# The first block's taps shared out anew, and the transposes and transfers of blocks 2 and 3 moved, in a dynamic convolution followed by a two-layer product

## The chip, the cores and the metric

One Trainium2 chip, one of its eight cores. The metric is the time of one execution on the device in microseconds (us), as the median of several runs; a profile is one more execution, recorded instruction by instruction.

## The reference

x is (4, 4096, 192), weight_gen (4, 4096, 8, 7), w_in (192, 2048), w_out (2048, 192), all float32.

```
w   = softmax(weight_gen) over its 7 taps
out[b, s, h, :] = sum over k of w[b, s, h, k] * x[b, s + k - 6, h, :]     (zeros ahead of s = 0)
h   = out @ w_in                                   # 16384 tokens, 192 -> 2048
g   = h where h >= 1, 0 where h <= -1, (h + 1)^2 / 4 between
result = g @ w_out                                 # 2048 -> 192
```

## The kernel before, in words

**Blocks and pairs.** The 16384 tokens are cut into 32 blocks of 512. A block's convolution gives a tile with tokens on partitions (128 partitions, 4 tokens each, 192 channels); gemm1 wants channels on partitions, so the block is transposed and split into a rounded part hc and a rest hl (`split_x`, L256). gemm1 makes 128 columns of d_ff at a time, gemm2 sums over them. One step is one such slice of 128, and the program is written in pairs of steps: a block has 8 pairs, and the loop over w (L600) has 256 pairs of gemm1 (`gemm1_pair`, L373) and, LAGP = 2 pairs later, as many of gemm2 (`gemm2_part`, L418, two parts for each pair). Pair w = 8 is the first of block 1, w = 16 of block 2, w = 24 of block 3.

**Between the two products** ScalarE and VectorE make g from a step's sums: `relu` and `square` (ScalarE, L398, L401), `act_g` (VectorE, L406), `split_g` (ScalarE gh L412, VectorE gl L413). gemm1's sums lie in four PSUM banks of the pool ps_h, two for each pair; a bank is free when split_g has read it.

**The order of the work** is written out by hand (`tc.manual_schedule`): each engine does its instructions in program order. `at(w, op, place=p)` (L478) puts an operation into pair w. In program order a pair is gemm1, place 5, gemm2, relu and square of its first step, place 0, relu of the second, place 9, square of the second and act_g of the first, places 10 and 1, act_g of the second, the evacuation's copies, place 2, split_g of both, places 13 and 4 (L600 to L651).

**SP's queue** issues all the transfers and has a second task. In `gemm2_part` a bank passes from one half of the rows to the other, and the matmul that takes it over waits for a no-op on SP (L443) that itself waits for the matmul before. The no-ops stand on SP in program order with the transfers: a transfer that waits there holds the no-ops behind it, and so gemm2.

**The first block** (L539 to L581). `softmax(0)`, then `conv_summed(0)` (L217): KV = 3 taps are summed on VectorE with PSUM as the accumulator and end in a piece, four taps are single products of GpSimd, a piece each. A piece is a tile of 192 channels with the first 64 repeated behind by ScalarE (`again`, L168), so that channels can be read as two neighbouring halves in any of three ways. TensorE turns each piece (`turn_sum`, L267; 12 turns for one piece, 4 for each of 3 chunks of channels) and sums the five pieces in PSUM (src). `drive(n, bank)` (L206) lets TensorE do n matmuls of 512 columns on the identity that nobody reads.

**The weights** come in eight chunks and are decoded (rounded high part and rest): `load_weights(c)`, `size(c)` on ScalarE (L328), `decode(c)`: VectorE mag (L360), head (L362) and two merges (L341), then ScalarE high and VectorE low for each half (L353, L357). Chunk c is needed by pair w = c; chunks 2 to 7 are decoded in pairs 1 to 6. Block 1's convolution on GpSimd is held back behind those decodings (L587), and it is turned by TensorE too (pair 7).

**Blocks 2 and on** (L513 to L537). `conv(b, nc.gpsimd)` has 13 operations on GpSimd (7 products, L179, and 6 adds, L189). `transpose_out(b)` (L275) has five operations: VectorE transposes acc into T (L289), a store D <- T to DRAM (L291), and for each of three chunks of channels a gather of two transfers XT <- D (L286). `split_out(b)` has ScalarE's hc (L262) and GpSimd's hl (L263) for each chunk. Their places are given as lists of (pair, place); for block b they count from w = (b - 2) * 8. For blocks 2 and 3 the transpose is at (w+11, place 2), the store at (w+12, 0), the gathers at (w+12, 4), (w+13, 0), (w+13, 4), the splits at (w+14, 0), (w+14, 4), (w+15, 0). For the others the first four stand at w+8 to w+12.

**The end.** `evac(b)` (L449) adds the two halves of a block's sums in two turns (ScalarE L457, VectorE L458 each), and one store writes the block (L466).

Of the kernel before, what the change touches and what calls it, by code (L numbers as in the profile page):

```python
# [10 lines left out]
F32 = mybir.dt.float32  # L11
# [10 lines left out]
def kernel(  # L22
# [22 lines left out]
    P = 128  # L45
# [9 lines left out]
    E = H * K  # L55
    R = D // 32
    LAGP = 2
    KV = 3


    n = 4
# [38 lines left out]
    def run(ops):  # L100
        for o in ops:
            o()
# [57 lines left out]
    SYNC = mybir.DependencyInfo(mybir.DependencyClass.Sync, mybir.DependencyReason.DATA)  # L160

    def whole():
        return op.tile([P, n, D + Q], F32, tag="piece", name="piece", bufs=K - KV + 1)

    def heads(t):
        return t[:, :, 0:D].rearrange("p j (h g) -> p j h g", h=H)

    def again(t):  # L168
        nc.scalar.activation(out=t[:, :, D:D + Q], in_=t[:, :, 0:Q], func=AF.Copy)
# [47 lines left out]
    def conv_summed(b):  # L217

        g, gi = group_of[b]
        wt, xtile = w_t[g], x_t.pop(b)  # L220
        near = ps_o.tile([P, 2, 512], F32, tag="o1", name="near")
        wn = near[:, 0, 0:n * E].rearrange("p (j h k) -> p j h k", j=n, h=H)
        sums = ps_o.tile([P, 2, 512], F32, tag="o0", name="sums")
        acc = sums.rearrange("p a d -> p (a d)")[:, 0:n * D].rearrange("p (j h g) -> p j h g", j=n, h=H)
        nc.scalar.activation(out=wn, in_=wt[:, gi], func=AF.Copy)

        def times(eng, out, w, k):
            return eng.tensor_tensor(
                out=out, in0=xtile[:, k:k + n, :].rearrange("p j (h g) -> p j h g", h=H),
                in1=w[:, :, :, k:k + 1].to_broadcast([P, n, H, G]), op=ALU.mult)  # L230

        own, pooled = [whole()], []

        def add(k):
            t = cv.tile([P, n, H, G], F32, tag="T", name="tap")
            times(nc.vector, t, wn, k)
            out = acc
            if k == KV - 1:
                out = heads(own[0])
            nc.vector.tensor_tensor(out=out, in0=acc, in1=t, op=ALU.add)  # L240
            if k == KV - 1:
                again(own[0])

        def alone(k):
            t = whole()
            pooled.append(t)
            times(nc.gpsimd, heads(t), wt[:, gi], k)
            again(t)

        return ([lambda: times(nc.vector, acc, wn, 0)] + [lambda k=k: add(k) for k in range(1, KV)],  # L250
                [lambda k=k: alone(k) for k in range(KV, K)], pooled, own)


    xT_t, xs_t, lows = {}, {}, []
# [39 lines left out]
    def split_out(b, eng):  # L294
        XT = xs_t.pop(b)
        return split_x(b, [XT[:, c].rearrange("p a n -> p (a n)") for c in range(NC)], eng)
# [76 lines left out]
    def gemm1_pair(w):  # L373

        b, f = steps[2 * w]
        hc, hl = xT_t[b]
        if w == 0:
            pair = [ps_o.tile([P, 2, 512], F32, tag=f"o{m}", name="psh0")[:, 0] for m in range(2)]
        else:
            pair = [ps_h.tile([P, 512], F32, tag="h", name="psh") for _ in range(2)]  # L380
        passes = []
        for l, r in ((whi, hc), (wlo, hc), (whi, hl)):
            passes += [(l, r, c) for c in range(NC)]
        for s, (l, r, c) in enumerate(passes):
            for h in range(2):
                rows = slice(h * Q, (h + 1) * Q)
                nc.tensor.matmul(out=pair[h][:, 0:N], lhsT=l[rows, f // 2, c], rhs=r[rows, (c - h) % NC if b < 2 else c],  # L387
                                 start=(s == 0), stop=(s == len(passes) - 1))
        for h in range(2):
            h_t[2 * w + h] = pair[h]  # L390
# [58 lines left out]
    def evac(b):  # L449

        t0 = b * N
        osb = op.tile([P, 4, D], F32, tag="osb", name="osb")
        pos = o_t.pop(b)
        by_turn = osb.rearrange("p (k m) d -> p m k d", m=n // 2)
        ops = []
        for m in range(n // 2):
            ops.append(lambda m=m: nc.scalar.activation(out=by_turn[:, m], in_=pos[m][:, :, D:2 * D], func=AF.Copy))  # L457
            ops.append(lambda m=m: nc.vector.tensor_tensor(  # L458
                out=by_turn[:, m], in0=pos[m][:, :, 0:D], in1=by_turn[:, m], op=ALU.add))

        def store():
            rows = out[t0:t0 + N, :]
            if b < 2:
                nc.sync.dma_start(out=rows.rearrange("(p j) d -> p (j d)", j=n), in_=osb.rearrange("p j d -> p (j d)"))
            else:
                nc.sync.dma_start(out=rows.rearrange("(a q) d -> q a d", q=P), in_=osb)  # L466

        return ops, store

# [11 lines left out]
    def later(make, where):  # L481

        ops = []
        for k, (w, place) in enumerate(where):
            if k == 0:
                at(w, lambda: ops.extend(make()), place=place)
            at(w, lambda k=k: ops[k](), place=place)
# [25 lines left out]
    for b in range(2, NB):  # L513
        w = (b - 2) * NP
        at(max(w - 5, 2), lambda b=b: clear_x(b))
        at({2: 3, 3: 8, 4: 11}.get(b, w - 3), lambda b=b: load_x(b), place=4 if b == 4 else 2)
        if b in first and b > 2:
            g = first[b]
            at(max(w - 9, NP - 1), lambda g=g: load_w(g))
            if b == 3:  # L520
                where = [(10, 4), (11, 2), (12, 0), (12, 4), (12, 4), (12, 4), (13, 2)]
            else:
                where = [(w - 6 + k, 4) for k in range(7)]
            later(lambda g=g, b=b: softmax(g, nc.gpsimd if b == 3 else nc.vector), where)
        if b == 2:
            where = [(6, 2)] * 2 + [(7 + k // 3, 2) for k in range(2 * K - 3)]
        else:
            z, d = (13, 3) if b == 3 else (w + CONV, 2)
            where = [(z + k // d, 2) for k in range(2 * K - 1)]
        later(lambda b=b: conv(b, nc.gpsimd), where)  # L530
        turned = [(TOUT, 2)] + [(TOUT + k, 0) for k in range(1, 2 + NC)]
        where = [(SPLIT + k // 4, (0, 0, 4, 4)[k % 4]) for k in range(2 * NC)]
        if b < 4:
            turned = [(11, 2), (12, 0), (12, 4), (13, 0), (13, 4)]
            where = [(14, 0)] * 2 + [(14, 4)] * 2 + [(15, 0)] * 2
        later(lambda b=b: transpose_out(b), [(w + k, place) for k, place in turned])
        later(lambda b=b: split_out(b, nc.gpsimd), [(w + k, place) for k, place in where])  # L537

    with tc.manual_schedule():  # L539
        nc.gpsimd.memset(warm, 0.0)  # L540
# [8 lines left out]
        clear_x(1)  # L549
        s0, s1 = softmax(0), softmax(1, nc.gpsimd)  # L550
        marks = [o() for o in s0[0:3] + s1[0:2] + s0[3:]]
        load_weights(0, marks[-1])
        load_weights(1)
        load_x(1)
        load_weights(2)
        load_weights(3)
        run(s1[2:4])
        v_ops, p_ops, pooled, own = conv_summed(0)
        src = [ps_h.tile([P, 512], F32, tag="h", name="psx") for _ in range(NC)]
        idle = ps_h.tile([P, 512], F32, tag="h", name="idle")  # L560
        drive(10, idle, marks[1])
        run(p_ops[0:3])
        run(v_ops)
        size(0)
        run(p_ops[3:])
        run(s1[4:6])
        for k, t in enumerate(pooled[0:3]):
            for c in range(NC):
                turn_sum(src, t, k == 0, False, c)
            drive(1, idle)  # L570
        d_ops, moves = decode(0)
        for c in range(NC):
            turn_sum(src, own[0], False, False, c)
            turn_sum(src, pooled[3], False, True, c)
        run(d_ops[0:3])
        splits = split_x(0, src, nc.vector)
        scaled = s1[6]()
        tc.add_manual_dep(scaled.ins, dec_last[0].ins.name, SYNC, reason="the decoding of a chunk goes first")
        run(splits[0:1] + splits[2:3] + moves[0:1] + splits[1:2] + splits[4:5] + moves[1:2] + splits[3:4] + splits[5:6])
        run(d_ops[3:])  # L580
        run(moves[2:4])  # L581
        size(1)
        e_ops, e_moves = decode(1)
        at(0, *e_ops, place=0)
        move(0, e_moves)
        turned1 = whole()
        n_ops = conv(1, nc.gpsimd, lambda k: dec_last.get(1 + k // 2), turned1)  # L587
        for k in range(2 * K - 1):
            at(k // 2, n_ops[k], place=1)
        at(NP - 2, lambda: again(turned1), place=4)  # L590
        at(0, lambda: drive(14, ps_h.tile([P, 512], F32, tag="h", name="idle")), place=5)
        at(1, lambda: drive(12, ps_o.tile([P, 2, 512], F32, tag="o0", name="idle")[:, 0]), place=5)
        src1 = []

        def turn1(c):
# [4 lines left out]
        for w in range(NS // 2 + LAGP):  # L600
# [29 lines left out]
            else:  # L630
# [11 lines left out]
                run(side.pop((w, 1), []))  # L642
                if i < NS:
                    act_g(j)
                run(copies)
                run(side.pop((w, 2), []))
                if i < NS:
                    split_g(i)
                    split_g(j)
            for place in (13, 4):  # L650
                run(side.pop((w, place), []))  # L651
            if store and i >= NS:
                store()
        assert not side, side


# [28 lines left out]
```

## Time and profile before

| | |
|---|---|
| runs (three), median | 1179.7 us (1177.17 to 1182.65) |
| the profiled execution, its own time | 1180.91 us |
| its span, first to last instruction | 1179.1 us |
| mean granted TensorE clock | 0.996 |
| busy: TensorE, ScalarE, VectorE, GpSimd | 1155.3, 969.5, 839.1, 797.8 us |

Busy time is time with an instruction at work, however slowly it moves. PE is TensorE's matmuls, DVE VectorE, ACT ScalarE, POOL GpSimd, SPq the queue of SyncE. A start time counts from the first instruction of the span.

### The profile page before, as it was taken

How to read it: one execution, taken by the hardware profiler on the slowest of the kernel's cores; microseconds unless marked ns; L12 is line 12 of the kernel's file. 1: busy time of each engine (PE TensorE's matmuls, PEld its weight loads, DVE VectorE, ACT ScalarE, POOL GpSimd, SP SyncE). 2: the span in 40 equal slices, each digit the busy share in tenths (PEclk: the TensorE clock that was granted, in tenths of full speed). 3: DMA queues.
4: the chain of work that ended last, by engine and by line, in shares of the span. 5: the costliest groups of instructions: out<-in, count | busy, mean ns of one | idle time of the engine just before them, and what ended most of it. 6: DMA issues, size and time to landing. Idle time of an engine off the chain costs nothing.

```text
span 1179.1 us, 32263 instructions
## 1 busy us (share of the span) xinstructions
PE 1155.3 (98%) x12911; PEld 1040.2 (88%) x12911; DVE 839.1 (71%) x1275; ACT 969.5 (82%) x1746; POOL 797.8 (68%) x514
## 2 busy tenths in 40 slices
PE   8898999999999999999999999999999999999998
PEld 5687889999999999999999999999999999999997
DVE  7975677767677776777767677676777767667665
ACT  5876788888888888888888888888888888888886
POOL 4586878586668848677685767858667785866410
PEclk9999999999999999999999999999999999999999
DMA  9312222122222122212122221212221222221100
GB/s 227 100 56 83 76 67 81 64 83 89 88 63 79 67 73 96 89 59 83 67 87 75 88 85 59 86 67 82 89 89 62 72 73 76 92 89 55 46 19 20
DMA packets 84038, 91.45 MB, mean 78 GB/s; under 512 B 5040, under 2 KB 75696, under 8 KB 83888
## 3 DMA queue, kind: packets, MB, share of 16 engines
q1 hardware_dynamic: 83888, 89.39, 23.5%
q8 instruction: 102, 1.67, 0.6%
q14 instruction: 48, 0.39, 0.1%
HBM read 64.99 MB, written 24.38 MB: 76 GB/s over the span
## 4 chain that ended last, share of the span: by engine, by line
PE 92%; DVE 3%; ACT 2%; DMA 1%; POOL 1%; issue 1%; SPq 0%; POOLq 0%; DVEq 0%
PE o L434 47%; PE psh L387 44%; PE psx L271 1%; DVE psh L406 1%; DMA D<-T 1%; DVE psw L341 1%; DVE head L362 1%; ACT mag L328 1%; DMA x<-in_x_dram 0%; POOL hl L263 0%; DVE wlo L357 0%; ACT u L398 0%; ACT hc L262 0%; POOL acc L189 0%; ACT u L401 0%
## 5 line engine op out<-in xcount | busy, mean ns | idle before, releaser
L434 PE MATMUL o<-wo,gh 64*128 64x384 f32 x4096 | 604.6, 355 | 4.7 <-SPq L443 4.7
L406 DVE SCALAR_TENSOR_TENSOR psh<-u,psh 128x512 f32<-128x512 f32 x512 | 354.6, 696 | 310.4 <-ACT u L401 310.3
L434 PE MATMUL o<-wo,gl 64*128 64x192 f32 x4096 | 525.5, 251 | 0.0
L434 PEld LDWEIGHTS o<-wo,gl 64*128 64x128 f32 x4096 | 398.1, 188 | 10.9
L434 PEld LDWEIGHTS o<-wo,gh 64*128 64x128 f32 x4096 | 392.3, 184 | 15.7 <-SPq L443 5.2
L398 ACT ACTIVATE u<-psh 128x512 f32<-128x512 f32 x512 | 301.9, 590 | 105.8 <-PE psh L387 104.1
L413 DVE TENSOR_TENSOR gl<-psh,gh 128x512 fp32r<-128x512 f32 x512 | 345.4, 686 | 15.1 <-ACT gh L412 0.7
L412 ACT ACTIVATE gh<-psh 128x512 fp32r<-128x512 f32 x512 | 299.7, 593 | 65.5 <-DVE psh L406 65.3
L189 POOL TENSOR_TENSOR acc<-acc,pr 128x768 f32<-128x768 f32 x185 | 342.5, 1851 | 2.3
L401 ACT ACTIVATE u<-u 128x512 f32<-128x512 f32 x512 | 323.6, 632 | 16.0
L179 POOL TENSOR_TENSOR pr<-x,w 128x768 f32<-128x768 f32 x186 | 286.2, 1546 | 18.8 <-DVE psw L341 14.0
L263 POOL TENSOR_TENSOR hl<-XT,hc 128x512 fp32r<-128x512 f32 x90 | 115.3, 1294 | 210.7 <-ACT hc L262 210.7
L387 PE MATMUL psh<-hc,whi 64*128 64x512 f32 x1536 | 232.9, 402 | 7.3 <-DVE wlo L357 6.7
L387 PE MATMUL psh<-hl,whi 64*128 64x512 f32 x1536 | 222.9, 390 | 2.6 <-POOL hl L263 2.6
L387 PE MATMUL psh<-hc,wlo 64*128 64x512 f32 x1536 | 224.9, 394 | 0.0
L387 PEld LDWEIGHTS psh<-hl,whi 64*128 64x128 f32 x1536 | 147.0, 184 | 36.8 <-POOL hl L263 3.8
L387 PEld LDWEIGHTS psh<-hc,wlo 64*128 64x128 f32 x1536 | 148.3, 186 | 34.3
L387 PEld LDWEIGHTS psh<-hc,whi 64*128 64x128 f32 x1536 | 128.7, 187 | 24.3 <-DVE wlo L357 6.2
L179 POOL TENSOR_TENSOR acc<-x,w 128x768 f32<-128x768 f32 x31 | 47.9, 1546 | 83.2 <-DVE w L155 75.9
L262 ACT ACTIVATE hc<-XT 128x512 fp32r<-128x512 f32 x90 | 55.7, 618 | 0.0
L289 DVE STREAM_TRANSPOSE T<-acc 128x768 f32<-128x768 f32 x30 | 50.9, 1698 | 0.0
L458 DVE TENSOR_TENSOR osb<-o,osb 128x384 f32<-128x384 f32 x64 | 32.8, 555 | 2.3 <-ACT osb L457 2.3
(44 smaller groups left out, 214.4 us busy)
## 6 DMA issues: line engine op xcount, KB each, us to landing
x<-in_x_dram SPq DMA_DIRECT2D x28, 960.0 KB
XT<-D SPq DMA_DIRECT2D x180, 128.0 KB
out_dram<-osb SPq DMA_DIRECT2D x32, 384.0 KB
D<-T SPq DMA_DIRECT2D x30, 384.0 KB
x<-in_x_dram SPq DMA_DIRECT2D x4, 945.0 KB
w<-in_weight_gen_dram SPq DMA_DIRECT2D x15, 224.0 KB
r<-in_moe_w_in_dram SPq DMA_DIRECT2D x16, 192.0 KB
r<-in_moe_w_out_dram SPq DMA_DIRECT2D x8, 384.0 KB
```

The source lines that it names most:

```text
L179: held(eng.tensor_tensor(out=t, in0=xtile[:, k:k + n, :].rearrange("p j (h g) -> p j h g", h=H), in1=wt[:, gi, :, :, k:k + 1].to_broadcast ...
L189: held(eng.tensor_tensor(out=o, in0=s, in1=t, op=ALU.add))
L262: ops.append(lambda c=c: nc.scalar.activation(out=hc[:, c], in_=src[c], func=AF.Copy))
L263: ops.append(lambda c=c: lows.append(eng.tensor_tensor(out=hl[:, c], in0=src[c], in1=hc[:, c].bitcast(F32), op=ALU.subtract)))
L289: lambda: nc.vector.transpose(out=T.rearrange("p b c j -> p b j c"), in_=acc.rearrange("p j (r b) -> p b j r", b=R)),
L387: nc.tensor.matmul(out=pair[h][:, 0:N], lhsT=l[rows, f // 2, c], rhs=r[rows, (c - h) % NC if b < 2 else c], start=(s == 0), stop=(s == len ...
L398: nc.scalar.activation(out=u_t[i], in_=h_t[i][:, 0:N], func=AF.Relu, scale=0.5, bias=0.5)
L401: nc.scalar.activation(out=u_t[i], in_=u_t[i], func=AF.Square)
L406: nc.vector.scalar_tensor_tensor(out=pv, in0=uv, scalar=1.0, in1=pv, op0=ALU.min, op1=ALU.max)
L412: nc.scalar.activation(out=gh[:, 0:N], in_=gv, func=AF.Copy)
L413: nc.vector.tensor_tensor(out=gl[:, 0:N], in0=gv, in1=gh[:, 0:N].bitcast(F32), op=ALU.subtract)
L434: mm = nc.tensor.matmul(out=o_t[b][turn][:, k, 0:cols], lhsT=l[rows, t * P:(t + 1) * P], rhs=wo[rows, f].rearrange("p s d -> p (s d)")[:, ...
```

## The change

In the first block VectorE makes one tap (tap 0) as a product alone and sums three (taps 1 to 3); GpSimd makes three (taps 4 to 6). The five pieces are turned one after the other, with no drive between them, behind 16 drives instead of 10. The weights' first transfer waits for the softmax's exponential instead of its last product. size(1) and part of the decoding of chunks 0 and 1 change their places in the order; the 14 drives behind pair 0 go, ten stand ahead of pair 1's matmuls, six instead of twelve behind them. For blocks 2 and 3 transpose, store, gathers and splits stand half a pair to a pair sooner, and block 3's convolution is spread differently; block 4's convolution, transpose and transfers stand one pair later. The stores of blocks that are evacuated after the last gemm1 go out in two halves.

```diff
-    KV = 3
+    KV = 4
...
     def whole():
-        return op.tile([P, n, D + Q], F32, tag="piece", name="piece", bufs=K - KV + 1)
+        return op.tile([P, n, D + Q], F32, tag="piece", name="piece", bufs=5)
...
-        own, pooled = [whole()], []
+        def alone(eng, w, k):
+            t = whole()
+            times(eng, heads(t), w, k)
+            again(t)
+            return t
 
         def add(k):
             t = cv.tile([P, n, H, G], F32, tag="T", name="tap")
             times(nc.vector, t, wn, k)
             out = acc
             if k == KV - 1:
+                own.append(whole())
                 out = heads(own[0])
             nc.vector.tensor_tensor(out=out, in0=acc, in1=t, op=ALU.add)
-            if k == KV - 1:
-                again(own[0])
-
-        def alone(k):
-            t = whole()
-            pooled.append(t)
-            times(nc.gpsimd, heads(t), wt[:, gi], k)
-            again(t)
-
-        return ([lambda: times(nc.vector, acc, wn, 0)] + [lambda k=k: add(k) for k in range(1, KV)],
-                [lambda k=k: alone(k) for k in range(KV, K)], pooled, own)
+
+        own = []
+        return alone, wn, wt[:, gi], lambda: times(nc.vector, acc, wn, 1), add, own
...
+        if w == 1:
+            drive(10, pair[0])
         passes = []
...
-        def store():
+        def store(m=None):
             rows = out[t0:t0 + N, :]
...
+            elif m is None:
+                nc.sync.dma_start(out=rows.rearrange("(a q) d -> q a d", q=P), in_=osb)
             else:
-                nc.sync.dma_start(out=rows.rearrange("(a q) d -> q a d", q=P), in_=osb)
+                nc.sync.dma_start(out=rows.rearrange("(k m q) d -> q m k d", q=P, m=n // 2)[:, m], in_=by_turn[:, m])
...
             if b == 3:
-                where = [(10, 4), (11, 2), (12, 0), (12, 4), (12, 4), (12, 4), (13, 2)]
+                where = [(10, 4), (11, 2), (12, 0), (12, 4), (12, 4), (12, 4), (12, 4)]
...
+        elif b == 3:
+            where = [(13 + k // 2, 2) for k in range(6)] + [(16, 2)] * 3 + [(17, 2)] * 2 + [(18, 2)] * 2
         else:
-            z, d = (13, 3) if b == 3 else (w + CONV, 2)
-            where = [(z + k // d, 2) for k in range(2 * K - 1)]
+            where = [(w + CONV + (b == 4) + k // 2, 2) for k in range(2 * K - 1)]
         later(lambda b=b: conv(b, nc.gpsimd), where)
-        turned = [(TOUT, 2)] + [(TOUT + k, 0) for k in range(1, 2 + NC)]
-        where = [(SPLIT + k // 4, (0, 0, 4, 4)[k % 4]) for k in range(2 * NC)]
+        z = w + (b == 4)
+        turned = [(z + TOUT, 2)] + [(z + TOUT + k, 0) for k in range(1, 2 + NC)]
+        where = [(w + SPLIT + k // 4, (0, 0, 4, 4)[k % 4]) for k in range(2 * NC)]
         if b < 4:
-            turned = [(11, 2), (12, 0), (12, 4), (13, 0), (13, 4)]
-            where = [(14, 0)] * 2 + [(14, 4)] * 2 + [(15, 0)] * 2
-        later(lambda b=b: transpose_out(b), [(w + k, place) for k, place in turned])
-        later(lambda b=b: split_out(b, nc.gpsimd), [(w + k, place) for k, place in where])
+            turned = [(w + 11, 0), (w + 11, 0), (w + 12, 0), (w + 12, 0), (w + 13, 0)]
+            where = [(w + 13, 4)] * 2 + [(w + 14, 0)] * 2 + [(w + 14, 4)] * 2
+        later(lambda b=b: transpose_out(b), turned)
+        later(lambda b=b: split_out(b, nc.gpsimd), where)
...
-        load_weights(0, marks[-1])
+        load_weights(0, marks[2])
...
-        v_ops, p_ops, pooled, own = conv_summed(0)
+        alone, near, far, second, add, own = conv_summed(0)
         src = [ps_h.tile([P, 512], F32, tag="h", name="psx") for _ in range(NC)]
-        idle = ps_h.tile([P, 512], F32, tag="h", name="idle")
-        drive(10, idle, marks[1])
-        run(p_ops[0:3])
-        run(v_ops)
+        drive(16, src[0], marks[1])
+        pieces = [alone(nc.vector, near, 0), alone(nc.gpsimd, far, KV)]
+        second()
+        pieces.append(alone(nc.gpsimd, far, KV + 1))
+        add(2)
+        pieces.append(alone(nc.gpsimd, far, KV + 2))
         size(0)
-        run(p_ops[3:])
+        add(3)
+        again(own[0])
+        pieces.append(own[0])
+        size(1)
+        for k, t in enumerate(pieces):
+            for c in range(NC):
+                turn_sum(src, t, k == 0, k == len(pieces) - 1, c)
+        d_ops, moves = decode(0)
+        run(d_ops[0:3])
         run(s1[4:6])
-        for k, t in enumerate(pooled[0:3]):
-            for c in range(NC):
-                turn_sum(src, t, k == 0, False, c)
-            drive(1, idle)
-        d_ops, moves = decode(0)
-        for c in range(NC):
-            turn_sum(src, own[0], False, False, c)
-            turn_sum(src, pooled[3], False, True, c)
-        run(d_ops[0:3])
         splits = split_x(0, src, nc.vector)
+        run(splits[0:1] + moves[0:1] + splits[1:2] + moves[1:2] + splits[2:3] + splits[4:5] + splits[3:4] + splits[5:6])
         scaled = s1[6]()
...
-        run(splits[0:1] + splits[2:3] + moves[0:1] + splits[1:2] + splits[4:5] + moves[1:2] + splits[3:4] + splits[5:6])
-        run(d_ops[3:])
-        run(moves[2:4])
-        size(1)
         e_ops, e_moves = decode(1)
-        at(0, *e_ops, place=0)
-        move(0, e_moves)
+        at(0, d_ops[3], *e_ops, place=0)
+        at(0, moves[2], e_moves[0], e_moves[2], place=9)
+        at(0, moves[3], e_moves[1], e_moves[3], place=10)
...
-        at(0, lambda: drive(14, ps_h.tile([P, 512], F32, tag="h", name="idle")), place=5)
-        at(1, lambda: drive(12, ps_o.tile([P, 2, 512], F32, tag="o0", name="idle")[:, 0]), place=5)
+        at(1, lambda: drive(6, ps_o.tile([P, 2, 512], F32, tag="o0", name="idle")[:, 0]), place=5)
...
-                run(copies)
+                if i < NS:
+                    run(copies)
+                else:
+                    for m in range(n // 2 if store else 0):
+                        run(copies[2 * m:2 * m + 2])
+                        store(m)
...
-            if store and i >= NS:
-                store()
```

## Rows read from the trace of the kernel before

**Rows 1.** Chain of waits in order of time, from pair 8: start us, us, what.

```profile
69.75 2.30 PE psh L387 x17
...
91.83 0.10 PE psh L387
...
92.02 4.21 DMA D<-T
...
134.10 3.83 DMA D<-T
...
156.25 2.12 PE psh L387 x18
...
1165.30 2.12 PE psh L387 x18
```

**Rows 2.** Waits between 60 and 160 us: us in total, times, longest.

```profile
PE o L434 <- SPq L443: 4.7, 2, 2.4
...
PE psh L387 <- POOL hl L263: 2.6, 3, 1.4
```

**Rows 3.** Windows: busy us (instructions) by engine, PEclk, DMA share, GB/s.

```profile
97.50:101.75 4.25, 4.15 (x28) 3.69 (x30) 0.83 (x2) 0.11 (x1) 4.00 (x3) 0.60 0.32 94
101.75:106.14 4.39, 4.39 (x52) 3.99 (x52) 1.16 (x2) 3.35 (x6) 1.56 (x2) 1.00 0.31 88
```

**Rows 4.** The page's groups of GpSimd: busy us, mean ns, idle before.

```profile
L189 POOL TENSOR_TENSOR acc<-acc,pr 128x768 f32<-128x768 f32 x185 | 342.5, 1851 | 2.3
...
L179 POOL TENSOR_TENSOR pr<-x,w 128x768 f32<-128x768 f32 x186 | 286.2, 1546 | 18.8 <-DVE psw L341 14.0
L263 POOL TENSOR_TENSOR hl<-XT,hc 128x512 fp32r<-128x512 f32 x90 | 115.3, 1294 | 210.7 <-ACT hc L262 210.7
```

**Rows 5.** Timeline of GpSimd: start us, us, then what; idle before in brackets.

```profile
81.24 3.79 POOL L189 TENSOR_TENSOR acc<-acc,pr 128x768 f32<-128x768 f32 x2
...
95.91 0.97 POOL L155 TENSOR_TENSOR w<-w,s 128x448 f32<-128x448 f32 x1 [9.15 <-DVE s L154]
```

**Rows 6.** Timeline of VectorE in pairs 10 and 11.

```profile
85.10 0.61 DVE L149 TENSOR_REDUCE m<-w 128x64 f32<-128x448 f32 x1
...
88.12 1.66 DVE L289 STREAM_TRANSPOSE T<-acc 128x768 f32<-128x768 f32 x1
```

**Rows 7.** The gathers of tile XT on SP's queue: ns min/median/max, first and last start.

```profile
L286 SPq DMA_DIRECT2D XT<-D x180: 573/602/1933, 96.2 to 1122.2; - x180
```

**Rows 8.** Timeline of TensorE in the head.

```profile
3.73 4.43 PE L209 MATMUL idle<-ident 128*128 128x512 bf16 x10 [3.73 <-DVE w L150]
8.78 2.82 PE L271 MATMUL psx<-ident,piece 128*128 128x128 f32 x12 [0.62 <-POOL piece L228]
...
15.41 2.78 PE L271 MATMUL psx<-ident,piece 128*128 128x128 f32 x24
...
31.73 1.41 PE L387 MATMUL psh<-hc,whi 64*128 64x512 f32 x6 [1.06 <-DVE wlo L357]
```

**Rows 9.** Chain of waits in order of time, decoding of the first chunks.

```profile
21.02 0.90 ACT mag L328
...
25.04 0.46 DVE wlo L357
...
27.09 0.90 ACT mag L328
...
33.18 0.90 ACT mag L328
```

**Rows 10.** Timeline of GpSimd, VectorE and ScalarE in the first block.

```profile
7.18 6.04 POOL L228 TENSOR_TENSOR piece<-x,w 128x768 f32<-128x768 f32 x4 [1.57 <-DMA x<-in_x_dram]
...
10.87 0.96 DVE L240 TENSOR_TENSOR piece<-sums,tap 128x768 f32<-128x768 f32 x1
...
12.76 0.91 ACT L328 ACTIVATE mag<-r 128x768 bf16<-128x768 bf16 x1 [0.28 <-DMA r<-in_moe_w_out_dram]
```

**Rows 11.** Timeline of SP's queue, the last transfer.

```profile
1175.42 0.38 SPq L466 DMA_DIRECT2D out_dram<-osb  x1
```

## The prediction

> **What bounds the kernel now.** I read the engines' shares first (the table above): TensorE is busy nearly all the time. The reader should not take that as "nothing to gain", because busy is not the same as advancing at full pace. So the next view is the chain of waits in order of time [rows 1]. From the start of pair w=25 (156.25) to that of w=255 (1165.30) lie 230 pairs in 1009.05 us, 4.387 us each, and nothing but matmuls is on the chain: that part cannot become shorter by moving work about. From w=8 (69.75) to w=25 lie 17 pairs, which at 4.387 would take 74.6 us and take 86.5: **11.9 us are lost there**. The waits of that stretch say where [rows 2]: TensorE waits twice for an SP no-op (longest 2.4 us) and three times for hl of GpSimd. Both waits for SP begin behind a D store (92.02 and 134.10 [rows 1]): a gather waits on SP for the store to land, 4.21 and 3.83 us, and the no-ops that release the next half of gemm2 stand behind it. After such a gap the granted clock is low: 0.60 of full over 97.50 to 101.75 [rows 3]; at the lower level of 0.5 that makes 3.4 us at 1.2 GHz, some 1.7 us of matmul work. Before w=8 the chain is another one: turns of the first block, then decoding, which repeats every 6.09 us (27.09 to 33.18) [rows 9] while TensorE needs 4.39.
>
> **Part 1, the first block up to its last turn (call that moment E).** Now E is 15.41 + 2.78 = 18.19 [rows 8]. The change takes one product from GpSimd (four run 7.18 to 13.22 [rows 10], so 1.5 us) and gives VectorE a product (about 0.96, as its adds [rows 10]): six operations of 0.96 from 7.2 end at 12.9, and ScalarE's copy of the last piece follows by 13.5. The pieces are not the limit, TensorE is: ten drives take 4.43 (0.44 each), the first twelve turns 2.82 (0.235 each), the last 24 turns 2.78 (some 0.11 each) [rows 8]. The pace doubled between them, though TensorE had a gap of 0.62 after the drives. With 16 drives and no gap I bound the drives' end: all at the lower pace, 3.73 + 16 x 0.44 = 10.8; half of them at the doubled pace, 9.0. I take the middle, 9.9. Sixty turns at 0.109 are 6.5, so E = 16.4 (15.5 to 17.3; if the first twelve still go at the lower pace and the drives end late, 18.9). **Gain 1.8.** The three single drives between the sets go; their cost is in E. The weights' transfers are issued some 2.4 us sooner; chunk 0 landed just before 12.76, when ScalarE took it up [rows 10], so it is there in time for size(0) near 12.2 and the gain beyond that is nothing. They follow x on SP's queue; should they delay x, E moves by less than 0.5, as it hangs on the drives and not on x.
>
> **Part 2, from E to the decoding loop.** From E to size(2) at 27.09 now lie 8.9 us, and VectorE's decoding of chunk 1 in them waits for size(1) of ScalarE [rows 9]: 0.90 from 21.02, after a wait of some 0.4; then VectorE's head, merges, act_g, two lows and act_g follow. The change does size(1) under the turns, which takes 1.3 out, and puts one low (0.46, the row at 25.04 [rows 9]) into the chain: **gain 0.85**. Splitting hc0 and whi in another order gains nothing: hc2, which ends last, stays last. The ten drives before pair 1 cost nothing, since TensorE would wait there for whi of chunk 1; the cover is that wait, and without it they would cost 2.2. The 14 drives of pair 0 go. Behind pair 1 six drives stand instead of twelve. The idle time there was 1.06 (the row at 31.73 [rows 8]); six drives fewer add 1.3 and the shortened chain before pair 1's matmuls 0.8, so **some 3.2 us of idle time arise**, more than the 2.4 after which the clock fell [rows 2, 3]. I expect a fall there. Its 1.7 us of lost work lie beside 1.0 to 1.7 of slack in the 6.09 us loop: I charge 0.6 (0 if the clock holds, 2.5 if the fall lasts twice as long).
>
> **Part 3, blocks 2 and 3** (times as if the head had not moved; pair 13 starts at 91.83). Block 2: GpSimd's last add ends at 85.03 [rows 5], VectorE's max at 85.71 [rows 6], so the transpose moved to place 0 runs 85.7 to 87.4 (1.66 each [rows 6]). Behind it wait act_g and split_g of pair 11, 1.0 late, which pair 13 needs only at 91.8. SP gets to the D store after pair 11's no-ops, at 87.45, ahead of load_x(4), which now queues behind it at no cost. The store lands by 91.7; the first two gathers, now together behind pair 12's no-ops, issue four transfers of 0.60 [rows 7], to 94.3. Pair 13's second half needs its no-ops at 95.1. **The first wait goes**, with 0.8 to spare, and so does the fall behind it. GpSimd's order becomes softmax multiply (to 96.88, as now [rows 5]), two products, hl0, hl1, product, add, hl2. With 1.55, 1.85 and 1.29 [rows 4] hl2 ends at 107.25; pair 16 wants it at 106.9: 0.35 lost.
>
> Block 3: the nine convolution operations left (four products, five adds, 15.4) end at 122.7, but pair 19 starts at 118.5. **This is what is late next**: the transpose at place 0 waits on VectorE until 122.7, and pair 19's act_g, which waits behind it, ends by 126, just before pair 21 wants the banks. D is issued at 124.4 and lands near 128.4; gathers go to 130.8, and pair 21's second half wants its no-ops at 130.5. I charge 0.7 (0.3 to 1.0). Block 4's first eight operations, hl0, hl1, two more, and hl2 then end at 143.25 against 143.0 wanted: 0.25. In all 1.3 of the 11.9 remain: **gain 10.6** (6.6 if one wait still grows to 2.4 and costs a fall of the clock, together over 4; 11.9 if none is left). The softmax multiply of block 3 keeps its neighbours on GpSimd: nothing. Block 4's transpose and gathers come one pair later; its last gather may make ScalarE wait half a microsecond, once, covered by the pair it is ahead.
>
> **Part 4, the tail.** The last store is issued at 1175.42 [rows 11], and the span ends 3.7 later. Half of it now goes one VectorE add sooner: **gain 0.5** (0 to 1.0; the bytes are the same, one issue more).
>
> **The sum**: 1.8 + 0.85 - 0.6 + 10.6 + 0.5 = 13.2 off the profiled execution's 1180.9, so 1167.7. That execution is 1.2 above the median; I leave that in the range.
>
> **A rule that speaks against the gap-free turns.** The row of the last turns [rows 8] shows 0.11 each for 24 in a row after a single drive, so in this kernel turns ran, and kept running, at the doubled pace. The Trainium skill, in "TensorE: Matmul & The Clock Gate", section "Part 4: PE-mode transpose", says that transposes do not count as activity in the way matmuls do and that the full clock does not engage for them. By that rule the turns would all go at the lower pace once the drives between them are gone, the first rival below.
>
> **The rivals.**
> - *The turns stay at the lower pace.* Sixty at 0.235 are 14.1 instead of 6.5: 7.6 more, 1175.3. For it: the first twelve, which followed drives. Against it: the last 24. Chance 0.08.
> - *GpSimd becomes the bound of blocks 2 and 3, or SP's gathers still hold the no-ops.* One D store lands 1.5 later, or VectorE reaches a transpose later: one old wait and one fall stay, 4 more, 1171.7 (to 1175). For it: margins of 0.3 to 0.8. Chance 0.15, two thirds of it still faster.
> - *Slower: the clock falls in the new gap behind pair 1 and stays down while decoding lasts.* Pairs 2 to 7 then need 8.77 instead of 6.09: 6 x 2.7 = 16.1, less the 0.6 charged, 1183.2. Each pair beyond the seventh costs 4.4 more, so one suffices for clearly slower; it decides from five pairs on. Against it: at half clock TensorE would be busy without a pause, and after the falls of today the clock came back in such a stretch [rows 3]. Chance 0.04.
> - *Something the trace of before does not show in the head* (a bank that is not free, a late transfer): 0.03, slower.
>
> **How the numbers follow.** The forecast has 0.70. A measurement of this kernel can tell about 0.5% from no change, 5.9 us: faster is below 1173.8, slower above 1185.6. Faster: 0.70 + 0.10; same: 0.05 of the second rival, 0.08 of the first and 0.02 of the third; slower: 0.02 + 0.03. The forecast's own bounds are 1164.4 (all gains at their best) and, with the larger charges, 1172; the run-to-run difference takes the low end to 1163.5, and the second rival the high end to 1174.5.
>
> **What the changed profile would show.** Turns that end near 16.4, twelve in some 1.3; size(2) near 24.5; a gap of some 3 us behind pair 1 and a low granted clock after it; no wait of gemm2 for SP over 1 us; transpose of block 3 waiting for GpSimd; waits for hl of some tenths each; pairs of 4.387 from w=25 on, which starts 11 to 13 sooner. The prediction is wrong if a wait for SP of 2 us is left, if turns take 0.235 throughout, or if pairs 2 to 7 take over 6.5 each.

## The result, and the profile after

The changed kernel takes 1169.0 us (median of five runs, 1168.41 to 1170.81); the kernel before, beside it, 1179.03. The ratio is 0.9918 (95% interval 0.9896 to 0.9940): faster by 0.8%. The profiled execution took 1170.06 with a span of 1168.3, 10.8 below that of before.

Where the span went, stretch by stretch (E is the end of the first block's last turn, size(2) the start of ScalarE's first step for chunk 2, pairs by the start of gemm1), all from one execution of each:

| stretch | before | after | change | forecast |
|---|---|---|---|---|
| start to E | 18.19 | 16.85 | -1.34 | -1.8 |
| E to size(2) | 8.90 | 8.13 | -0.77 | -0.85 |
| size(2) to pair 8 | 42.66 | 43.47 | +0.81 | +0.6 |
| pair 8 to pair 25 | 86.50 | 76.36 | -10.14 | -10.6 |
| pair 25 to pair 255 | 1009.05 | 1009.92 | +0.87 | 0 |
| pair 255 to the end | 13.80 | 13.57 | -0.23 | -0.5 |
| span | 1179.1 | 1168.3 | -10.80 | -13.15 |

The chain of waits in order of time after the change, to set beside [rows 1]:

```profile
68.45 2.31 PE psh L386 x17
...
129.47 0.02 SPq L442
...
144.81 2.12 PE psh L386 x18
...
149.20 2.16 PE psh L386 x18
...
153.89 2.31 PE psh L386 x17
...
158.42 1.74 PE psh L386 x14
...
1154.73 2.12 PE psh L386 x18
```

Both pieces "DMA D<-T" have left the chain. Pair 25 starts 11.44 sooner, pair 255 10.57 sooner. The waits between 56 and 160 us, beside [rows 2]:

```profile
PEld psh L386 <- POOL hl L260: 1.5, 2, 0.9
...
DVE T L286 <- POOL acc L189: 1.2, 1, 1.2
...
PE psh L386 <- POOL hl L260: 0.7, 2, 0.4
...
PEld psh L386 <- DVE gl L412: 0.4, 1, 0.4
```

TensorE's matmuls no longer wait for an SP no-op in this list, hl costs 0.7 instead of 2.6, and there are two new waits: VectorE's transpose of block 3 for GpSimd, and a weight load for gl. GpSimd and VectorE where [rows 5, 6] showed them, then VectorE, with its rows 37 and 66 us later:

```profile
79.89 3.79 POOL L189 TENSOR_TENSOR acc<-acc,pr 128x768 f32<-128x768 f32 x2
...
94.64 0.98 POOL L155 TENSOR_TENSOR w<-w,s 128x448 f32<-128x448 f32 x1 [9.15 <-DVE s L154]
```

```profile
84.35 1.76 DVE L286 STREAM_TRANSPOSE T<-acc 128x768 f32<-128x768 f32 x1
...
121.37 1.73 DVE L286 STREAM_TRANSPOSE T<-acc 128x768 f32<-128x768 f32 x1 [1.17 <-POOL acc L189]
...
150.01 1.01 DVE L457 TENSOR_TENSOR osb<-o,osb 128x384 f32<-128x384 f32 x2
150.94 1.75 DVE L286 STREAM_TRANSPOSE T<-acc 128x768 f32<-128x768 f32 x1
152.57 1.27 DVE L412 TENSOR_TENSOR gl<-psh,gh 128x512 fp32r<-128x512 f32 x2
```

The last three rows are the price of block 4's later transpose: in pair 25 VectorE also evacuates block 2, so gl ends at 153.84, pair 27 starts 4.69 after pair 26 instead of 4.39, and pair 28 another 4.53 later (158.42): 0.45 in all. TensorE in the head, beside [rows 8], and the clock around the gap behind pair 1, beside [rows 3]:

```profile
3.79 6.51 PE L209 MATMUL psx<-ident 128*128 128x512 bf16 x16 [3.79 <-DVE w L150]
10.14 6.71 PE L268 MATMUL psx<-ident,piece 128*128 128x128 f32 x60
...
29.52 1.97 PE L386 MATMUL psh<-hc,whi 64*128 64x512 f32 x6 [2.77 <-DVE wlo L354]
```

```profile
26.75:29.50 2.75, 0.00 (x0) 0.00 (x0) 2.72 (x6) 2.29 (x6) 1.01 (x1) 1.00 1.10 188
30.25:33.50 3.25, 3.25 (x18) 2.50 (x18) 2.98 (x6) 1.42 (x2) 1.58 (x1) 0.50 0.05 13
```

Sixty turns without a drive between them take 6.71. Behind pair 1 TensorE is idle for 2.77, and then the granted clock is 0.50, 1.2 GHz. At the start of the span the granted clock in the windows is 1.00 even where one drive takes over 0.4, so what is said below of the pace in the first block goes by the time of one instruction.

### The profile page after: what moved, and what is told of

Same layout as the page of the kernel before. It is cut to its first block, busy times and chain, and to the rows that moved or that the text cites. A ratio compares the mean times of both kernels' runs of the same rounds, so it can differ in the third digit from the quotient of the medians.

```text
span 1168.3 us, 32247 instructions
## 1 busy us (share of the span) xinstructions
PE 1150.9 (99%) x12904; PEld 1058.3 (91%) x12904; DVE 838.4 (72%) x1276; ACT 968.7 (83%) x1746; POOL 796.2 (68%) x513
## 4 chain that ended last, share of the span: by engine, by line
PE 94%; DVE 3%; ACT 1%; POOL 1%; issue 1%; DMA 0%; DVEq 0%; SPq 0%
PE o L433 47%; PE psh L386 45%; PE psx L268 1%; DVE psh L405 1%; DVE psw L338 1%; PE psx L209 1%; DVE head L359 1%; POOL hl L260 0%; ACT mag L325 0%; POOL acc L189 0%; DVE wlo L354 0%; ACT u L397 0%; POOL pr L179 0%; DVE mag L357 0%; DMA w<-in_weight_gen_dram 0%
## 5 line engine op out<-in xcount | busy, mean ns | idle before, releaser
L433 PE MATMUL o<-wo,gh 64*128 64x384 f32 x4096 | 619.7, 355 | 0.2
L433 PE MATMUL o<-wo,gl 64*128 64x192 f32 x4096 | 560.1, 251 | 0.0
L433 PEld LDWEIGHTS o<-wo,gh 64*128 64x128 f32 x4096 | 462.4, 184 | 9.3 <-SPq L442 0.6
L433 PEld LDWEIGHTS o<-wo,gl 64*128 64x128 f32 x4096 | 459.7, 187 | 7.2
L386 PE MATMUL psh<-hc,whi 64*128 64x512 f32 x1536 | 249.1, 402 | 8.2 <-DVE wlo L354 7.1
L386 PE MATMUL psh<-hc,wlo 64*128 64x512 f32 x1536 | 241.9, 395 | 0.0
L386 PE MATMUL psh<-hl,whi 64*128 64x512 f32 x1536 | 240.0, 391 | 0.7 <-POOL hl L260 0.7
L386 PEld LDWEIGHTS psh<-hc,wlo 64*128 64x128 f32 x1536 | 168.8, 186 | 27.1
L386 PEld LDWEIGHTS psh<-hl,whi 64*128 64x128 f32 x1536 | 166.8, 185 | 28.4 <-POOL hl L260 1.5
L386 PEld LDWEIGHTS psh<-hc,whi 64*128 64x128 f32 x1536 | 147.2, 186 | 22.7 <-DVE wlo L354 8.8
```

What stands on the lines that cost most here:

```text
L433: mm = nc.tensor.matmul(out=o_t[b][turn][:, k, 0:cols], lhsT=l[rows, t * P:(t + 1) * P], rhs=wo[rows, f].rearrange("p s d -> p (s d)")[:, ...
```

## The experiments

Each stretch of the table is touched by different edits, so one profile of a kernel answers several questions; pairs are read from the chain of waits. The kernels with twelve drives, with the weights late again and with two drives ran once each, so only stretches of their profiles are read.

**The places of blocks 2, 3 and 4 alone**: the kernel before with the changed lists from `if b == 3:` to `later(lambda b=b: split_out(...))`.

```diff
-                where = [(10, 4), (11, 2), (12, 0), (12, 4), (12, 4), (12, 4), (13, 2)]
+                where = [(10, 4), (11, 2), (12, 0), (12, 4), (12, 4), (12, 4), (12, 4)]
...
+        elif b == 3:
+            where = [(13 + k // 2, 2) for k in range(6)] + [(16, 2)] * 3 + [(17, 2)] * 2 + [(18, 2)] * 2
         else:
-            z, d = (13, 3) if b == 3 else (w + CONV, 2)
-            where = [(z + k // d, 2) for k in range(2 * K - 1)]
+            where = [(w + CONV + (b == 4) + k // 2, 2) for k in range(2 * K - 1)]
...
-            turned = [(11, 2), (12, 0), (12, 4), (13, 0), (13, 4)]
-            where = [(14, 0)] * 2 + [(14, 4)] * 2 + [(15, 0)] * 2
...
+            turned = [(w + 11, 0), (w + 11, 0), (w + 12, 0), (w + 12, 0), (w + 13, 0)]
+            where = [(w + 13, 4)] * 2 + [(w + 14, 0)] * 2 + [(w + 14, 4)] * 2
...
```

> The kernel before, with the new places for blocks 2, 3 and 4 alone (first block, weights, drives and tail as before). Theory (most of the gain is the two waits for SP and the wait for GpSimd between pairs 8 and 25): pair 8 starts near 69.75 as before, pair 25 near 146.1 instead of 156.25, the span is 1169.5 to 1170, about 9.5 us below before. Rival (the gain is the first block's, the new places only shift the waits to block 4 or later): pair 25 within 2 us of 156, span over 1176.

Measured: median 1171.14, ratio 0.9917 (0.9901 to 0.9934), span 1170.4; from its chain:

```profile
69.90 2.30 PE psh L387 x17
...
93.52 1.59 SPq L286
...
146.21 2.12 PE psh L387 x18
```

Pairs 8 to 25 take 76.31 instead of 86.50. The matmuls' waits for SP there are 1.0 in two pieces instead of 4.7, and each of the two stands behind the issue of one gather that took long (1.59 above, 1.27 at the second) where the others take some 0.6. The span is 0.4 above the expected 1170, and pairs 25 to 255 take 1010.13 instead of 1009.05. The theory holds: these lists alone bring nearly the whole gain. Which of the lists brings how much was not taken apart.

**All but these places**: the changed kernel with the old lists.

```diff
...
-            turned = [(w + 11, 0), (w + 11, 0), (w + 12, 0), (w + 12, 0), (w + 13, 0)]
-            where = [(w + 13, 4)] * 2 + [(w + 14, 0)] * 2 + [(w + 14, 4)] * 2
...
+            turned = [(11, 2), (12, 0), (12, 4), (13, 0), (13, 4)]
+            where = [(14, 0)] * 2 + [(14, 4)] * 2 + [(15, 0)] * 2
...
```

> The changed kernel with blocks 2, 3 and 4 placed as before (first block, weights, drives and tail as changed). Theory: pair 8 starts near 68.45, 1.3 sooner than before, the two gathers hold SP's no-ops again, pair 25 near 155, span 1177.5 (1 to 2 us below before; a measurement of the whole cannot tell it from no change). Rival: span near 1169.

Median 1175.96, ratio 0.9961 (0.9949 to 0.9973); the profiled execution has a span of 1177.4, pair 8 at 68.39 and pair 25 at 154.95, 86.56 apart, and the old waits are back:

```profile
PE o L433 <- SPq L442: 3.1, 2, 2.5
...
PE psh L386 <- POOL hl L260: 2.9, 3, 1.7
```

The stretches are as expected. The median gained 4.6, more than the 1.7 of the profiled span; that execution was the slowest of ten (the others had spans of 1172.5 to 1177.1). In which stretch the others were shorter was not recorded. Their mean granted clock was: it is 0.994 in the two longest (1177.4 and 1177.1) and 0.998 in the shortest (1172.5). Over some 1175 us this difference of 0.004 is 9.4 us at 1.2 instead of 2.4 GHz, an estimated 4.7 us of matmul work, about the whole 4.9 between them. Falls of the clock that some executions have and others do not would fit that; where they lay stays open. The two parts' medians (9.4 and 4.6) add up to more than the whole change brings.

**Twelve drives behind pair 1.**

```diff
-        at(1, lambda: drive(6, ps_o.tile(
+        at(1, lambda: drive(12, ps_o.tile(
```

> The changed kernel with twelve drives behind pair 1 again instead of six. Theory (the idle time of 2.77 us let the clock fall, and the fall cost 0.8): the gap shrinks to 1.4 to 1.6, the granted clock stays at 1.00 through pair 2, size(3) starts 12.2 us behind the start of size(2) plus one period instead of 13.0, pair 8 starts near 67.6 instead of 68.45. Rival (the fall lies beside VectorE's decoding and costs nothing): pair 8 starts within 0.2 of 68.45.

Span 1170.7, pair 8 at 70.04: against both expectations. The cause lies ahead of the edit: x landed late.

```profile
10.54 0.95 DVE L228 TENSOR_TENSOR piece<-x,near 128x768 f32<-128x768 f32 x1 [2.27 <-DMA x<-in_x_dram]
```

```profile
11.55 6.77 PE L268 MATMUL psx<-ident,piece 128*128 128x128 f32 x60 [2.58 <-DVE piece L228]
...
31.93 1.42 PE L386 MATMUL psh<-hc,whi 64*128 64x512 f32 x6 [1.49 <-DVE wlo L354]
```

In the stretch that the edit touches the theory holds: the gap is 1.49, the clock stays at 1.00, and from size(2) (27.39) to pair 8 are 42.65, as before the change and 0.82 less than in the changed kernel.

**The weights late again.**

```diff
-        load_weights(0, marks[2])
+        load_weights(0, marks[-1])
```

> The changed kernel with the weights' first transfer behind the softmax's last product again, as before the change. Theory (the sooner transfers are a condition of size(1) ahead of the splits): chunk 1 lands some 2.4 us later than now, near 16.7; ScalarE takes size(1) up near 16.7 and hc0 near 17.6 instead of 16.02, and pair 8 starts 1 to 1.6 us later, near 69.5 to 70. x lands near 7.2 instead of 7.7. Rival, the step of the prediction (the sooner transfers gain nothing beyond size(0)): pair 8 starts within 0.3 of 68.45.

Pair 8 started at 68.41, as the rival said, but not for its reason. ScalarE and TensorE:

```profile
15.81 0.88 ACT L325 ACTIVATE mag<-r 128x768 bf16<-128x768 bf16 x1 [1.63 <-DMA r<-in_moe_w_out_dram]
16.59 0.58 ACT L259 ACTIVATE hc<-psx 128x512 fp32r<-128x512 f32 x1
```

```profile
9.09 6.71 PE L268 MATMUL psx<-ident,piece 128*128 128x128 f32 x60
```

size(1) waited for chunk 1, and hc0 came at 16.59, although the first third of the turns' sums was whole near 15.0 (turns end at 15.80, and hc0 began 0.83 ahead of their end in the changed kernel). The wait cost 1.6. In this execution it is hidden by drives that took 5.44 instead of 6.51, so that E came 1.05 sooner, and by the way from size(2) to pair 8, which took 42.86 instead of 43.47. So size(1) ahead of the splits does need the sooner transfers.

**Two drives instead of sixteen.**

```diff
-        drive(16, src[0], marks[1])
+        drive(2, src[0], marks[1])
```

> The changed kernel with 2 drives ahead of the turns instead of 16. It asks whether turns alone bring the full pace. Theory (turns count as work): the first 12 to 36 turns take 0.235 each and the rest 0.11, so the 60 take between 8.2 and 11 us and end between 17 and 20 (the first piece is there near 8.7). Rival (the page's rule that the full clock does not engage for transposes): all 60 stay at 0.235, 14.1 us, ending near 22.8, and pair 0's matmuls begin at the lower pace too.

```profile
3.85 1.01 PE L209 MATMUL psx<-ident 128*128 128x512 bf16 x2 [3.85 <-DVE w L150]
8.89 8.47 PE L268 MATMUL psx<-ident,piece 128*128 128x128 f32 x60 [4.04 <-DVE piece L228]
...
19.10 1.08 PE L386 MATMUL psh<-hc,wlo 64*128 64x512 f32 x6
```

After 4.04 us of idle time, sixty turns and nothing else take 8.47: 0.141 each on average, between 0.235 and 0.11, and pair 0's six matmuls behind them take 1.08, as at the full clock (1.90 at 1.2 GHz, below). Turns alone bring TensorE to its full pace. The Trainium skill's sentence on transposes ("TensorE: Matmul & The Clock Gate", "Part 4: PE-mode transpose"), by which these would have taken 14.1, does not hold for these float32 turns. The fourteen drives are worth 0.5 against the changed kernel's profile, E at 17.36 against 16.85; against three profiles whose sixteen drives took 5.3 to 5.4 (E at 15.66 to 15.80) they are worth some 1.6.

**Three edits to what remained**:

```diff
-            ops.append(lambda c=c: lows.append(eng.tensor_tensor(
+            low = nc.vector if b in (2, 3) and c == NC - 1 else eng
+            ops.append(lambda c=c, low=low: lows.append(low.tensor_tensor(
...
-        turned = [(z + TOUT, 2)] + [...]
+        turned = [(z + TOUT + 1, 0) if b == 4 else (z + TOUT, 2)] + [...]
...
-        at(1, lambda: drive(6, ...
+        at(1, lambda: drive(12, ...
```

> The changed kernel with three edits that touch different stretches: twelve drives behind pair 1; the last hl of blocks 2 and 3 on VectorE instead of GpSimd; block 4's transpose at the start of pair 26 instead of the end of pair 25, where VectorE also evacuates block 2. Theory: from the start of size(2) to pair 8 some 42.65 instead of 43.47 (no fall of the clock); from pair 8 to pair 25 75.0 to 75.4 instead of 76.36 (no wait for hl, the transpose of block 3 waits less than 0.3 for GpSimd); pair 26 to 27 4.39 instead of 4.69. About 2 us in all below the changed kernel, 1166 to 1168 where the first turns begin at the same time. Rival (GpSimd is not the bound there, VectorE or SP is): the stretch from pair 8 to 25 stays within 0.3 of 76.36.

Median 1167.62, ratio 0.9901 (0.9883 to 0.9919), span 1165.2:

```profile
67.27 2.13 PE psh L387 x15
...
142.41 2.12 PE psh L387 x18
146.79 2.12 PE psh L387 x18
151.18 2.12 PE psh L387 x18
```

size(2) (24.59) to pair 8: 42.68. Pairs 8 to 25: 75.14. Pair 26 to 27: 4.39. All three as expected. Without the moved hl pairs 8 to 25 take 76.31 to 76.37 in six profiles, however long the matmuls wait for SP's no-ops in them (up to 1.0), so hl of GpSimd was the bound of the remainder. With it the stretch is not steady: in the two kernels built on this one (below) it took 75.61 and 76.15, the latter within the rival's 0.3. No matmul waits for hl in either, and SP's no-ops hold them for 0.6 and 0.8, so what is late next is SP. Another part missed: VectorE's transpose of block 3 still waits 1.15 for GpSimd, since VectorE reaches it sooner too.

**The changed kernel again**, with no edit.

> The changed kernel once more, for what differs between executions. Theory: the sixteen drives take between 5.2 and 6.5 us, the turns 6.7 once they begin; the gap behind pair 1 is 2.8 again and the clock falls again within it or just behind; pair 25 starts 76.4 behind pair 8. Rival: the stretch from pair 8 to 25 differs by over 0.5 between executions, so that the small remainders there cannot be read.

Median 1170.36, ratio 0.9915 (0.9901 to 0.9929), 2.7 above the three edits, whose runs stand beside it. Pairs 8 to 25 take 76.34 (69.93 to 146.27), so 0.3 can be read there. The head differs: x lands at 10.43, the drives take 5.17, and behind the same gap the clock does **not** fall:

```profile
28.93:31.70 2.77, 0.11 (x1) 0.00 (x0) 2.74 (x6) 2.31 (x6) 0.92 (x1) 1.00 0.75 157
31.70:34.20 2.50, 2.39 (x17) 1.80 (x19) 2.41 (x5) 1.88 (x4) 2.45 (x2) 1.00 0.04 15
```

**When the weights are sent**, on top of the three edits: behind the second w's mark, and (second kernel) behind the last mark.

```diff
-        load_weights(0, marks[2])
+        load_weights(0, marks[4])
```

```diff
-        load_weights(0, marks[2])
+        load_weights(0, marks[-1])
```

> e6_all_three with the weights' first transfer behind GpSimd's subtraction of the second softmax, so behind the landing of the second w, some 1.6 us later than in e6. It asks why x landed at 7.7 in four profiles of the changed head and at 10.4 to 10.5 in two. Theory (the weights' sooner transfers share the DMA engines with x and sometimes hold it up): x is there by 7.9 in the profile, and the five spans lie within 1.5 us of each other near 1165 to 1166.5, without one 3 us above the lowest, as e6 and the changed kernel have. size(1) waits for chunk 1 to some 14.8, which hides under the turns. Rival (x's landing has nothing to do with the weights): spread as in e6 (4.2 us).

> e6_all_three with the weights' first transfer behind the first softmax's last product, as in the kernel before. Theory: x is there by 7.7, the spans lie within 1.5 us of each other, but size(1) waits for chunk 1 to 15.8 and delays hc0 to 16.6 where the turns would allow some 15.0 to 15.2, so the lowest span is 0.5 to 1.6 above that of e8_weights_behind_w1. Rival: same lowest span as e8, so the sooner transfers gain nothing at all.

With `marks[4]` x is in use at 7.26, and the five spans are 1166.3 to 1167.3, where those of the three edits alone are 1165.2 to 1169.4: the spread went from 4.2 to 1.0, as the theory said, while the lowest is 1.1 higher. The median, 1168.23, ratio 0.9904 (0.9887 to 0.9922), cannot be told from 1167.62. Two things were not as expected. size(1) waited for chunk 1 to 15.35 and not to 14.8, so hc0 came at 16.14 and TensorE was idle for 1.48 behind the turns. And behind the gap of 1.50, with twelve drives ahead of it, the clock fell here too (granted 0.50 over 31.5 to 34.0):

```profile
29.64 1.42 PE L387 MATMUL psh<-hc,whi 64*128 64x512 f32 x6 [1.50 <-DVE wlo L355]
...
31.52 1.90 PE L387 MATMUL psh<-hl,whi 64*128 64x512 f32 x6
```

From size(2) to pair 8 it cost next to nothing (42.72). With `marks[-1]` the median is 1170.13, ratio 0.9921 (0.9904 to 0.9937), and the lowest span 1167.4, 1.1 above, as expected, but the spread is 4.2, which was not. In the profiled execution, the slowest, x is in use at 7.60, so x is not the only cause:

```profile
16.75 0.88 ACT L326 ACTIVATE mag<-r 128x768 bf16<-128x768 bf16 x1 [1.72 <-DMA r<-in_moe_w_out_dram]
17.54 0.58 ACT L259 ACTIVATE hc<-psx 128x512 fp32r<-128x512 f32 x1
```

```profile
18.55 0.79 PE L387 MATMUL psh<-hc,whi 64*128 64x512 f32 x1 [2.73 <-ACT whi L351]
19.52 1.64 PE L387 MATMUL psh<-hc,whi 64*128 64x512 f32 x5 [0.18 <-ACT hc L259]
20.54 1.90 PE L387 MATMUL psh<-hc,wlo 64*128 64x512 f32 x6
```

The late chunk leaves TensorE idle for 2.73 behind the turns, and pair 0 then runs at the lower pace (1.90 for six against 1.09).

## Why the prediction was right

The value (1167.7), the range (1163.5 to 1174.5) and the sign hold; the sum of 13.2 was too large by 2.4 against the profiled execution, and all six terms of the table missed on the same side, by 0.08 to 0.87. Term by term:

- **Blocks 2 and 3** (10.6 forecast, 10.14 measured, 10.19 by their lists alone): right, with its mechanism. No gather waits for its store on the chain any more, and SP's no-ops hold TensorE only for some tenths. The margin of 0.8 that was worked out for them took every issue of a gather at 0.60; in the seven of these waits (in five profiles) whose chain runs through the gathers, one issue took 1.19 to 1.59, so the margin was not there. What remains of 11.9 is 1.8 instead of 1.3. "What is late next" was named rightly: block 3's transpose waits for GpSimd (1.17), and hl comes late twice; moving one hl to VectorE took 1.2 of these 1.8 away in one profile, 0.75 and 0.2 in two others.
- **E** (1.8 forecast, 1.34): the mechanism was right (the drives' end, not the pieces, sets it), the drives were mis-sized: the turns begin at 10.14 rather than 9.9, and take 0.112 instead of 0.109. Across executions sixteen drives took 5.2 to 6.5, so they end between 9.0 and 10.3, within the bounds of 9.0 to 10.8. Where x was in time, E came between 15.66 and 16.85 with them.
- **E to size(2)** (0.85 forecast, 0.77): right.
- **The fall behind pair 1** (0.6 charged, 0.81): right in the first profile, but it is chance. The gap was 2.77 rather than 3.2. Behind a gap of 2.77 to 2.78 the way from size(2) to pair 8 was 43.47, 43.49, 42.86, 43.64 and 42.64 in five profiles, against 42.65 to 42.72 with twelve drives, in four profiles, one of them with a fall. The charge lies between 0 and 1.0. For a fall of twice the length the prediction had 2.5; the one of that length (two drives, some 6.8 us at 0.50) gave 43.64, 1.0 more.
- **The weights**: "the gain beyond that is nothing" failed. The step looked at size(0) and forgot that the change puts size(1) ahead of the splits; without the sooner transfers size(1) waits 1.6 to 1.7. It also put the price of a delayed x under 0.5, since E hung on the drives: where x landed near 10.4, E came at 18.2 to 18.3 instead of 16.85, or of 15.66 to 15.80 where the drives were nearly as short as there. That the weights delayed x is not shown.
- **Block 4's later transpose** was costed at nothing, and the cover named was ScalarE's. The cost came on VectorE: 0.30 in pair 26 and 0.14 in pair 27, gone in two of three profiles with that transpose moved (in the third the pairs from 25 on took 4.60 and 4.48; the cause is open). The rest of the 0.87 between pairs 25 and 255 lies in single pairs, from 504.97 on 4.77 and from 540.45 on 4.53, which are others in other executions; their cause was not looked for.
- **The tail** (0.5 forecast, 0.23): only the first half of the store goes one VectorE add sooner. The second waits for the second add, as the whole store did, and is issued 10.1 behind the start of pair 255, as before (1164.8 and 1175.42); only the way from there to the end is shorter, 3.5 instead of 3.7. From pair 255 to the end nine profiles with two halves took 13.3 to 13.8, the two with one store 13.8 and 14.1.

The first rival fell (turns at the lower pace). The second came true in tenths, not in 4 us. The third fell: the clock came back after 3.4 us, and after 6.8 us in the longest case.

## What to carry to other kernels

Read a queue that both moves data and passes signals on as an engine: each wait of a gather for its store cost TensorE some 4 to 5 us, because gemm2's releases stood behind it and the clock fell after the stop. Here the places that let the store go some 4 us sooner, half a pair further ahead of its gathers, removed both. When an operation is moved to a sooner place, list all that it reads: size(1) moved ahead made a transfer critical that had been free. After such a move look at what else its new neighbours do (an evacuation in the same pair), not only at what it waits for.

## What the runs showed of the hardware

The same program shows different heads from execution to execution. x was in use at 7.7 to 7.9 in four profiles with the weights sent at `marks[2]` and at 10.4 to 10.5 in two, and at 7.2 to 7.6 in the five measured with later weights; sending them behind the second w narrowed the spans from 4.2 to 1.0 us, sending them later still did not (4.2). That this is sharing of the DMA engines fits where x landed but was not shown by itself, and two late landings of six against none of five may be chance. The pace of TensorE rose within sixty transposes after four idle microseconds, with no matmul among them, and an idle time of 2.77 us was followed by 1.2 GHz in four of five profiles, one of 1.49 to 1.50 us in one of three.
